# A planner's order for ScalarE and VectorE: from hand-set slacks to deadlines worked back from TensorE

## The chip, the core and the metric

One core of a Trainium2 chip runs the kernel. TensorE multiplies, VectorE and ScalarE do the arithmetic between its products, GpSimd helps in the first third, and SP issues nearly all DMAs. The metric is the device time of one execution in microseconds; lower is better.

## The reference, cut to what matters

A causal attention with a decay feeds two feed-forward layers; the change lies in the second half of the kernel, in the layers.

```python
x = attn_out.transpose(0, 2, 1, 3).reshape(2304, 512)   # after the attention
h = x @ w_in                     # 512 -> 2048
x = (h - np.tanh(h)) @ w_out     # layer 0, 2048 -> 512
h = x @ w_in2
return (h * (1 / (1 + np.exp(-h)))) @ w_out2            # layer 1
```

The weights arrive as float64, and the kernel turns them into float32 on the chip.

## The kernel before

Each float32 operand is split into a high and a low part (`gr`, `xr`, `wh`/`wl`), and a product is three matmuls. Blocks of two by two are multiplied with seven products in place of eight (a Strassen-Winograd scheme), so sums of blocks are made on VectorE ahead of the products (the stages `f_a`, `f_b`, `f_12`, `f_21`, `f_22`) and of the weights (`ws`), and results are gathered in running sums in PSUM.

A *unit* is one of three blocks of 768 tokens with one of four sets of 512 hidden columns, in each of two layers: 24 units. The first three run in slots that are written out by hand; from 259 us on the function `joint` makes the rest. TensorE's order there is fixed: h step, a step, h step, a step. An h step (`h_step`, L656) multiplies an x block (`xr`) by the input weights into a PSUM bank `h`; an a step (`c_step`, L729, and `plain_c`, L769, for the three units of `PLAIN`) multiplies the bent hidden block (`gr`) by the output weights into a bank `a`. A unit has seven of each (eight a steps in a plain one), and its a steps run beside the next unit's h steps.

Between them stand, on ScalarE, the copies that seed one running sum with another (`h<-h` L937, `a<-a` L1016), the activations (L930, L933), the casts to the high parts (`gr` L980, `xr` L905, `wh` L247) and the scaling of raw weights (L203); on VectorE the low parts (`gr` L981, `xr` L902, `wl` L249), the sums of stages (L940), h - tanh(h) (L934), the decoding of weights (L207 to L230) and the results' sums (`x<-a,x` L1024). In the last set of layer 0 four more sums per unit (`mix`, L1047) read the bank `a` and mix quarters of x. `make` (L890 to L905) prepares the `xr` of layer 1 and spills them to DRAM.

`joint` only lists tasks: a due time in steps of TensorE, an engine (P TensorE, A ScalarE, V VectorE, S and D DMAs), a cost in steps, what is read and written, a flag `keen` and an addend `spare`. `planned` runs the list against a clock of its own: TensorE and the DMAs keep their order; VectorE and ScalarE take, whenever they come free, one of the tasks that are ready. The order in which tasks come out is the order in which instructions are issued, and each engine works through its own strictly. In the rule of before the task with the least `when + spare` is taken; a task that isn't keen gives way to a keen one that becomes ready while it would run:

```python
n = min(now, key=lambda n: tasks[n][7])
if not tasks[n][6] and tasks[n][7] > t - 2:
    soon = [r for r, k in known if tasks[k][6] and t < r < t + tasks[n][2] - 0.2]
```

SP issues the reloads of `xr` (L625), the spills (L638), the weights (L164) and `aside` (L673, L676), a block of sums parked in DRAM, in the order of the tasks that they stand behind.

Of the kernel before, what the change touches and what calls it, by code (L numbers as in the profile page):

```python
# [8 lines left out]
F32R = mybir.dt.float32r  # L9
# [5 lines left out]
P = 128  # L15
# [24 lines left out]
PLAIN = (12, 13, 14)  # L40
PLAINSETS = {u // NB for u in PLAIN if u >= NB * NSET}
EARLIER = 5
MIXED = {u // NB for u in PLAIN if u < NB * NSET}

# [4 lines left out]
def forgetting_attention_two_ffn(  # L49
# [106 lines left out]
    def wload(q, m, parts=(0, 1)):  # L156
# [20 lines left out]
    )  # L177
# [418 lines left out]
    def ftile(u, what):  # L596
        k = u % 2
        if what == "12":
            if "12" not in small_tiles:
                small_tiles["12"] = pools["xb"].tile([P, 2, 2, TH], F32, tag="xo7", name="f_12")  # L600
            return small_tiles["12"][:, k]
        if what == "21":
            return flat(f"21_{k}", "hp", f"h{k}")
        if what == "1":
            return flat("1", "tp", "t0")
        if what == "22":
            return flat("22", "tp", "t1")
        if what == "tmp":
            if what not in small_tiles:
                g = gfree.pop(0)  # L610
                small_tiles[what] = pools[f"gp{g // 2}"].tile([P, 2, TH], F32, tag=f"gh{g}", name="f_tmp")
                small_tiles["spare"] = g
            return small_tiles[what]
        return flat(what, "xt", {"a": "xt1", "b": "xt2"}[what])
# [49 lines left out]
    def aside_tile():  # L664

        if "tile" not in aside:
            g = small_tiles["spare"]
            aside["tile"] = pools[f"gp{g // 2}"].tile([P, 2, TH], F32, tag=f"gl{g}", name="aside")
        return aside["tile"]
# [40 lines left out]
    def c_step(u, k):  # L710
        l, i = units[u][0], csteps(u)[k]
        t = gtile(gop(u, k))
        if u in PLAIN:
            return plain_c(u, *i, t)
        acc, fresh = cbank(u, i)
        at = WAT[l][i]
        ws = [[w[:, 0] for w in place(2 * (u // NB) + j, at)] for j in range(2)]
        for d in range(3 if l else 2):
            ds = slice(d * P, d * P + P)
            for j, (wh, wl) in enumerate(ws):  # L720
                gh, gl = (t[:, e, j] for e in range(2))
                if l:
                    dst = acc[:, d // 2, 256 * (d % 2):256 * (d % 2) + 256]
                    terms = ((gh[:, ds], wh), (gh[:, ds], wl), (gl[:, ds], wh))
                else:
                    dst = acc[:, d, 0:TH]
                    terms = ((wh[:, ds], gh), (wh[:, ds], gl), (wl[:, ds], gh))
                for r, (w, m) in enumerate(terms):
                    nc.tensor.matmul(  # L729
                        dst, w, m, start=fresh and (l == 0 or d != 1) and j == r == 0,  # L730
                        stop=j == 1 and r == 2, skip_group_check=True,
                    )

    def place(q, at):

        if at >= 11:
            if q % NSLOT < 2:
                return [w[:, 7:8] for w in wtile(q, 0)]
            if "spare" not in wtiles:
                g = small_tiles["spare"]  # L740
                t = pools[f"gp{g // 2}"].tile([P, 2, 256], F32R, tag=f"gl{g}", name="wspare")
                wtiles["spare"] = [t[:, 0:1], t[:, 1:2]]
            return wtiles["spare"]
        return [w[:, at - 8:] for w in extra(q, 1)] if at >= 8 else [w[:, at:] for w in wtile(q, 1)]
# [5 lines left out]
    def plain_c(u, c, a, t):  # L750
# [4 lines left out]
        for d in range(2 - a if l else 2):  # L755
            for j in range(2):
                q = 2 * (u // NB) + j
                gh, gl = (t[:, e, j] for e in range(2))
                if l:
                    ds = slice((2 * a + d) * P, (2 * a + d) * P + P)  # L760
# [35 lines left out]
    def joint():  # L796
# [5 lines left out]

        def task(when, eng, cost, fn, reads=(), writes=(), keen=False, spare=0):

            tasks.append((when, eng, cost, fn, reads, writes, keen, when + spare))

# [16 lines left out]
        def decode(q, m):  # L823
# [17 lines left out]
            groups = [0, 1, 2] if m and q // 2 in MIXED else [0, 1]  # L841
            behind = m and q % 2 and 3 * (q // 2) - 1 in PLAIN
            for g in [1, 3, 4, 5] if behind else groups:
# [4 lines left out]
        def spread(t0, t1, jobs, since):  # L848
# [3 lines left out]
            for e, c, fn, r, w, tag in jobs:  # L852
                if e == "D":
                    task(t - 6, e, c, fn, r, w)
                    continue
                t = max(t, since.get((w[0][:3], tag), t))
                task(t, e, c, fn, r, w, False, 3)
                if e == "V":
                    t += (t1 - t0) * c / total
# [22 lines left out]
        def make(u):  # L882
# [6 lines left out]
            def total(when, to, p, r, op=MINUS):  # L889
                task(t0 + when, "V", W2, lambda: tt_(q[to](), q[p](), q[r](), op), (key[p], key[r]), (key[to],), False, 2)  # L890

# [4 lines left out]
            for k, i in enumerate(STEPS):  # L896
# [7 lines left out]

                task(when, "A", N2, lambda n=n, f=f: copy(ring_tile(n)[:, 0], q[f]()), (key[f],), (kr,), False, 2)  # L905
                task(when + 0.1, "V", W2, low, (key[f], kr), (kr,), False, 2)


        for u in range(U0, len(units) + 1):
            t0 = base[u]  # L910
            if u < len(units):
# [27 lines left out]
                def two(when, to, p, r, op, kt, kp, kr, keen=True):  # L939
                    task(when, "V", W2, lambda: tt_(to, p, r, op), (kp, kr), (kt,), keen, 0 if keen else 2.5)  # L940

# [34 lines left out]
                for k, i in enumerate(order):  # L976
                    n = opno(u) + k
                    g, (frm, kf), kg = gtile(n), src[i], n % 3
                    w = t0 + when[k] + (more if k else 0)
                    task(w, "A", N2, lambda g=g, f=frm: copy(g[:, 0], f), (kf,), (("gh", kg),), False, 2)  # L980
                    task(w + 0.1, "V", W2, lambda g=g, f=frm: tt_(g[:, 1], f, rd(g[:, 0]), MINUS),  # L981
                         (kf, ("gh", kg)), (("gl", kg),), False, 2)
            v = u - 1
# [19 lines left out]
            for k, i in enumerate(csteps(v)):  # L1003
                if plain_:
                    n, kd = gop(v, k), (ky, kz)[i[1]]
                    r = [kd, ("gh", n % 3), ("gl", n % 3)] + [w for j in range(2) for g in (range(1) if l else range(3)) for w in wkeys(q + j, 1, g)]
                    task(t0 + min(2 * k + 1, 14), "P", 1, lambda v=v, k=k: c_step(v, k), r, (kd,))
                    continue
# [3 lines left out]
                when = t0 + k if last else t0 + 2 * k + 1  # L1012
                task(when, "P", 1, lambda v=v, k=k: c_step(v, k), r, (kd,))

# [15 lines left out]
            if l == 0:  # L1030
# [14 lines left out]
                else:  # L1045
                    def mix(when, spare, to, frm, r, op, keys, kt):
                        task(when, "V", W2, lambda: tt_(to() if callable(to) else to, frm, r, op), keys, (kt,), False, spare)  # L1047

                    mix(t0 + 11.5, 4, aside_tile, xs[22], xs[21], MINUS, (kx[22], kx[21]), "aside")
                    mix(t0 + 12.5, 3, xs[22], xs[22], xs[12], PLUS, (kx[22], kx[12]), kx[22])  # L1050
                    mix(t0 + 14.05, 1.2, xs[12], xs[12], ys, MINUS, (kx[12], ky), kx[12])
                    mix(t0 + 14.06, 1.2, xs[21], xs[21], ys, PLUS, (kx[21], ky), kx[21])
                task(t0 + (14.5 if s < NSET - 1 else 13), "S", 0, lambda b=b: aside_store(b), ("aside",), (("t1", b),))
# [62 lines left out]
    def planned(tasks):  # L1116
# [12 lines left out]
        writer, readers, deps = {}, {}, []  # L1129
        for n, (when, eng, cost, fn, reads, writes, keen, due) in enumerate(tasks):  # L1130
            d = {writer[k] for k in reads if k in writer}
# [11 lines left out]
        queue = {e: [n for n, t in enumerate(tasks) if t[1] == e] for e in free}  # L1143

        def ready(n):
            if all(d in end for d in deps[n]):
                return max([end[d] + lag(n, d) for d in deps[n]] + [tasks[n][0] - EARLY])

        while any(queue.values()):
            best = None  # L1150
            for e, waiting in queue.items():
# [457 lines left out]
```

## Time and profile before

| | |
|---|---|
| median of 3 runs | 914.43 us (914.15 to 914.65) |
| the profiled execution, its span | 914.77 us, 913.0 us |
| TensorE busy | 897.7 us, 98% |
| VectorE busy | 771.3 us, 84% |
| ScalarE busy | 594.6 us, 65% |
| DMA, mean | 215 GB/s |
| TensorE's granted clock, mean | 0.996 |

Times in the rows are microseconds from the span's start. A clock of 1.00 is 2.4 GHz, 0.50 is 1.2 GHz. An instruction of VectorE lasts in its row longer than the distance to the next one's start, since neighbours overlap a little; sums over a queue go by the starts.

### The profile page before, as it was taken

Reading aid. Unit: us, or ns where it says so; the run is one execution under the profiler, and the core shown is the slowest. Engines: PE = TensorE matmul, PEld = TensorE weight load, DVE = VectorE, ACT = ScalarE, POOL = GpSimd, SP = SyncE. Lnnn points to the kernel's source line nnn. Section 1 sums busy time; section 2 is a strip of 40 time slices with the busy share of each in tenths; the row PEclk is TensorE's granted clock in tenths of the full one; section 3 lists DMA queues with packets and bytes.
Section 4 is the critical chain, followed back from the end, with each engine's and each line's share of the span. In section 5 each row is a group of like instructions: output and inputs, shape, how many; then the busy total and the mean of one; then the engine's idle time right before and its main releaser. Section 6 shows DMA issues by size and latency. Waiting matters only on the chain.

```text
span 913.0 us, 15853 instructions
## 1 busy us (share of the span) xinstructions
PE 897.7 (98%) x5898; PEld 842.2 (92%) x5898; DVE 771.3 (84%) x1297; ACT 594.6 (65%) x992; POOL 161.3 (18%) x242
## 2 busy tenths in 40 slices
PE   9999999999999999999999989999999999999997
PEld 6777777799999999999999979898899999999997
DVE  7799999789888999998999989875598889876647
ACT  5888888766565767666776767665565566555443
POOL 8999999400000000000000000000000000000000
PEclk9999999999999999999999989999999999999999
DMA  5424533567457777787768656676567666555753
GB/s 164 154 98 155 167 121 103 193 245 314 196 217 265 237 252 259 236 302 280 251 241 287 220 207 252 238 267 235 190 230 282 205 225 225 180 201 176 233 167 117
DMA packets 51101, 196.01 MB, mean 215 GB/s; under 512 B 9744, under 2 KB 15120, under 8 KB 50992
## 3 DMA queue, kind: packets, MB, share of 16 engines
q1 hardware_dynamic: 50744, 194.72, 60.2%
q8 instruction: 46, 0.75, 0.3%
q10 hardware_dynamic: 280, 0.28, 0.1%
q14 instruction: 31, 0.25, 0.1%
HBM read 151.98 MB, written 41.88 MB: 212 GB/s over the span
## 4 chain that ended last, share of the span: by engine, by line
PE 93%; DVE 4%; ACT 2%; issue 1%; POOL 0%; DVEq 0%; ACTq 0%; POOLq 0%
PE h L656 32%; PE a L729 28%; PE a L769 5%; PE s L1294 5%; PE t L1341 5%; PE a L431 5%; PE out_t L1397 5%; PE h L475 3%; PE s L1286 2%; PE h L461 1%; PE out_t L1425 1%; DVE x L1047 1%; DVE gr L981 0%; DVE x L1024 0%; PE out L1397 0%
## 5 line engine op out<-in xcount | busy, mean ns | idle before, releaser
L656 PE MATMUL h<-xr,wh 128*128 128x384 f32 x1176 | 299.8, 335 | 1.0 <-ACT h L937 0.9
L656 PEld LDWEIGHTS h<-xr,wh 128*128 128x128 f32 x1176 | 210.6, 189 | 3.4 <-ACT h L937 1.6
L656 PE MATMUL h<-xr,wl 128*128 128x384 f32 x588 | 197.0, 335 | 0.0
L656 PEld LDWEIGHTS h<-xr,wl 128*128 128x128 f32 x588 | 110.6, 188 | 0.0
L981 DVE TENSOR_TENSOR gr<-f,gr 128x768 fp32r<-128x768 f32 x102 | 97.0, 953 | 14.5 <-ACT gr L980 14.5
L980 ACT CAST gr<-f 128x768 fp32r<-128x768 f32 x102 | 85.5, 838 | 33.3 <-PE a L729 29.5
L1024 DVE TENSOR_TENSOR x<-a,x 128x768 f32<-128x768 f32 (+1 forms) x64 | 59.4, 930 | 28.2 <-PE a L729 27.7
L1315 ACT ACTIVATE p<-p,mn 128x128 f32<-128x128 f32 (+3 forms) x128 | 71.2, 558 | 17.1 <-DVE mn L1307 14.4
L729 PE MATMUL a<-wh,gr 128*128 128x256 f32 x420 | 80.8, 282 | 0.0
L729 PE MATMUL a<-gr,wh 128*128 128x384 f32 x288 | 75.2, 341 | 4.7 <-ACT a L1016 4.1
L1329 POOL TENSOR_SCALAR p<-p,sm 128x128 f32<-128x128 f32 (+3 forms) x128 | 72.7, 584 | 7.7 <-DVE sm L1326 7.2
L1307 DVE CUSTOM_DVE_ANT_0 p<-s,mask 128x128 f32<-128x128 f32 (+3 forms) x128 | 59.6, 479 | 14.3 <-PE s L1294 14.2
L729 PEld LDWEIGHTS a<-wh,gr 128*128 128x128 f32 x420 | 67.5, 190 | 0.0
L1016 ACT COPY a<-a 128x768 f32<-128x768 f32 x43 | 33.7, 784 | 41.8 <-PE a L729 38.5
L729 PE MATMUL a<-weh,gr 128*128 128x256 f32 x312 | 60.2, 282 | 0.3 <-DVE x L1024 0.3
L729 PE MATMUL a<-wl,gr 128*128 128x256 f32 x210 | 59.4, 283 | 0.6 <-DVE wl L249 0.6
L937 ACT COPY h<-h 128x768 f32<-128x768 f32 x42 | 32.9, 784 | 39.6 <-PE h L656 39.2
L729 PEld LDWEIGHTS a<-gr,wh 128*128 128x128 f32 x288 | 53.0, 191 | 5.9 <-ACT a L1016 4.8
L729 PE MATMUL a<-gr,weh 128*128 128x384 f32 x216 | 54.8, 334 | 0.0
L1236 POOL TENSOR_TENSOR kqs<-kqraw,kqs 128x288 fp32r<-128x288 f32 (+1 forms) x62 | 53.8, 889 | 1.3
L937 ACT COPY f<-h 128x768 f32<-128x768 f32 x42 | 33.7, 802 | 30.4 <-PE h L656 22.7
L729 PEld LDWEIGHTS a<-weh,gr 128*128 128x128 f32 x312 | 50.2, 190 | 0.6 <-issue 0.5
(167 smaller groups left out, 2106.3 us busy)
## 6 DMA issues: line engine op xcount, KB each, us to landing
xr<-xd SPq DMA_DIRECT2D x126, 768.0 KB
raw<-w_in SPq DMA_DIRECT2D x32, 512.0 KB
raw<-w_out SPq DMA_DIRECT2D x32, 512.0 KB
xd<-xo SPq DMA_DIRECT2D x21, 768.0 KB
xd<-xr SPq DMA_DIRECT2D x21, 768.0 KB
kqraw<-kq SPq DMA_DIRECT2D x16, 608.0 KB
aside<-aside SPq DMA_DIRECT2D x15, 384.0 KB
vraw<-v SPq DMA_DIRECT2D x16, 320.0 KB
```

The costliest lines, as they stand in the source:

```text
L431: nc.tensor.matmul(dst, w, m, start=first and r == 0, stop=last and r == 2)
L656: nc.tensor.matmul(dst[:, j, 0:TH], w[:, ds], m[:, d], start=i in (1, 5) and d == r == 0, stop=d == 1 and r == 2, skip_group_check=True,)
L729: nc.tensor.matmul(dst, w, m, start=fresh and (l == 0 or d != 1) and j == r == 0, stop=j == 1 and r == 2, skip_group_check=True,)
L769: nc.tensor.matmul(dst, w, m, start=fresh and j == r == 0, stop=last and j == 1 and r == 2, skip_group_check=True)
L937: task(when, "A", N2, lambda: copy(to, frm), (kf,), (kt,), True)
L980: task(w, "A", N2, lambda g=g, f=frm: copy(g[:, 0], f), (kf,), (("gh", kg),), False, 2)
L981: task(w + 0.1, "V", W2, lambda g=g, f=frm: tt_(g[:, 1], f, rd(g[:, 0]), MINUS), (kf, ("gh", kg)), (("gl", kg),), False, 2)
L1024: task(when, "V", n, lambda: tt_(to, *((frm, to) if op == PLUS else (to, frm)), op), (kf, kx[c]), (kx[c],), True)
L1236: eng.tensor_tensor(lo[:, c0:c1], raw[p][:, c0:c1], rd(hi[:, c0:c1]), ALU.subtract)
L1307: nc.vector.tensor_tensor_reduce(out=pt.rearrange("p (g c) -> p g c", g=2) if i == 4 else pt, in0=src, in1=m, op0=ALU.add, op1=ALU.min, sc ...
L1315: nc.scalar.activation(pt, pt, AF.Exp, bias=mn, scale=-1.0, accum_out=sums[:, n // 3 % 5, n % 3, 0:1],)
L1329: nc.gpsimd.tensor_scalar(pt, pt, sm[:, j:j + 1], 1.0, ALU.mult, ALU.mult)
```

## The change

Every task loses `spare`. `planned` works a latest start back from TensorE's tasks through all that depend on each other, takes the ready task with the least latest start, and lets an engine idle for a more urgent task that is about to be ready, if the chosen one could wait for it. `behind` is how late TensorE's last planned step is against its due time. `keen` stays only in the planned lag of a dependence. The other edits concern sets of units that are plain in part (`MIXED`), the place of their weights, and a name (`spare` becomes `aside`).

```diff
-PLAINSETS = {u // NB for u in PLAIN if u >= NB * NSET}
+PLAINSETS = {s for s in range(NSET, 2 * NSET) if all(NB * s + b in PLAIN for b in range(NB))}
-MIXED = {u // NB for u in PLAIN if u < NB * NSET}
+MIXED = {u // NB for u in PLAIN} - PLAINSETS
...
-        def task(when, eng, cost, fn, reads=(), writes=(), keen=False, spare=0):
+        def task(when, eng, cost, fn, reads=(), writes=(), keen=False):
 
-            tasks.append((when, eng, cost, fn, reads, writes, keen, when + spare))
+            tasks.append((when, eng, cost, fn, reads, writes, keen))
...
-                task(t, e, c, fn, r, w, False, 3)
+                task(t, e, c, fn, r, w)
...
-                    mix(t0 + 14.05, 1.2, xs[12], xs[12], ys, MINUS, (kx[12], ky), kx[12])
-                    mix(t0 + 14.06, 1.2, xs[21], xs[21], ys, PLUS, (kx[21], ky), kx[21])
+                    mix(t0 + 14.05, xs[12], xs[12], ys, MINUS, (kx[12], ky), kx[12])
+                    mix(t0 + 14.06, xs[21], xs[21], ys, PLUS, (kx[21], ky), kx[21])
...
+        latest = [t[0] if t[1] == "P" else 1e9 for t in tasks]
+        for n in reversed(range(len(tasks))):
+            for d in deps[n]:
+                if tasks[d][1] != "P":
+                    latest[d] = min(latest[d], latest[n] - lag(n, d) - tasks[d][2])
...
+        behind = 0
...
-                n = min(now, key=lambda n: tasks[n][7])
-                if not tasks[n][6] and tasks[n][7] > t - 2:
-                    soon = [r for r, k in known if tasks[k][6] and t < r < t + tasks[n][2] - 0.2]
-                    if soon:
-                        t = min(soon)
-                        n = min((k for r, k in known if r <= t and tasks[k][6]), key=lambda n: tasks[n][7])
+                n = min(now, key=lambda n: latest[n])
+
+                soon = [(r, k) for r, k in known if t < r < t + tasks[n][2] - 0.1 and latest[k] + behind < t + tasks[n][2]
+                        and latest[n] + behind > r + tasks[k][2]]
+                if soon:
+                    t, n = min(soon)
...
+            if e == "P":
+                behind = t - tasks[n][0]
```

In the orders below L numbers are those of each kernel's own file, and names carry their buffer and tile numbers. The first place is the turn from layer 0 to layer 1, 523 to 531 us. `x_69<-x_69,a0` are the two `mix` sums that read the bank, `gr0` is the low part that an a step waits for, `xr64` to `xr66` are blocks of layer 1. VectorE before:

```order
L934 TENSOR_TENSOR f_21_1_3814<-h1_3809,f_21_1_3814 128x768
L902 TENSOR_TENSOR xr64_6064<-x_69,xr64_6064 128x768
L890 TENSOR_TENSOR f_tmp_4038<-x_69 128x768
L940 TENSOR_TENSOR f_a_3815<-f_12_3812,f_1_3811 128x768
L1047 TENSOR_TENSOR aside_4345<-x_69 128x768
L940 TENSOR_TENSOR f_12_3812<-f_22_3813,f_12_3812 128x768
L1047 TENSOR_TENSOR x_69<-x_69,a0_3795 128x2x384
L1047 TENSOR_TENSOR x_69<-x_69 128x2x384
L902 TENSOR_TENSOR xr65_6134<-f_tmp_4038,xr65_6134 128x768
L1047 TENSOR_TENSOR x_69<-x_69,a0_3795 128x2x384
```

VectorE now:

```order
L912 TENSOR_TENSOR xr64_6065<-x_69,xr64_6065 128x768
L1058 TENSOR_TENSOR x_69<-x_69 128x2x384
L944 TENSOR_TENSOR f_21_1_3814<-h1_3809,f_21_1_3814 128x768
L944 TENSOR_TENSOR f_12_3812<-f_12_3812,f_tmp_4039 128x768
L1058 TENSOR_TENSOR x_69<-x_69,a0_3795 128x2x384 x2
L900 TENSOR_TENSOR f_tmp_4039<-x_69 128x768
L991 TENSOR_TENSOR gr0_3817<-f_21_1_3814,gr0_3817 128x768
L950 TENSOR_TENSOR f_a_3815<-f_12_3812,f_1_3811 128x768
L950 TENSOR_TENSOR f_b_3816<-f_22_3813,f_a_3815 128x768
L912 TENSOR_TENSOR xr65_6156<-f_tmp_4039,xr65_6156 128x768
```

The two sums that read `a0` stand now next to each other, three rows behind `f_21_1`, where they stood six and nine rows behind it, and `f_a` stands behind them. ScalarE at the same place, before:

```order
L937 COPY h1_3809<-h0_3810 128x2x384
L905 CAST xr65_6134<-f_tmp_4038 128x768
L905 CAST xr66_6140<-x_69 128x768
L980 CAST gr2_3819<-f_a_3815 128x768
L930 ACT_TABLE_LOAD
L930 ACTIVATE f_1_3811<-h1_3809 128x768
L905 CAST xr67_6162<-x_69 128x768
L1016 COPY a0_3795<-a1_3802 128x2x384
L980 CAST gr1_3818<-f_b_3816 128x768
```

ScalarE now:

```order
L947 COPY h1_3809<-h0_3810 128x2x384
L915 CAST xr66_6139<-x_69 128x768
L1027 COPY a0_3795<-a1_3802 128x2x384
L915 CAST xr65_6156<-f_tmp_4039 128x768
L940 ACT_TABLE_LOAD
L940 ACTIVATE f_1_3811<-h1_3809 128x768
L990 CAST gr1_3818<-f_b_3816 128x768
L990 CAST gr2_3819<-f_a_3815 128x768
```

`a0<-a1` stood behind the table load and two more, and stands now ahead of the table load. The second place is the end of the plain units, 650 to 657 us, on ScalarE; `wh2_1` are weight blocks of the a steps to come, `x_69<-a0` and `x_69<-a1` are results of the last plain unit. Before:

```order
L930 ACTIVATE f_21_1_3814<-h1_3809 128x768
L980 CAST gr1_3818<-f_21_1_3814 128x768
L1065 COPY x_69<-a1_3802 128x2x256
L1065 COPY x_69<-a0_3795 128x2x512
L980 CAST gr2_3819<-f_b_3816 128x768
L247 CAST wh2_1_3854<-ws11_1_6862 128x256
L937 COPY h1_3809<-h0_3810 128x2x384
L247 CAST wh2_1_3854<-ws11_1_6862 128x512
L247 CAST wh2_1_3854<-ws11_1_6862 128x256
```

Now:

```order
L940 ACTIVATE f_21_1_3814<-h1_3809 128x768
L990 CAST gr1_3818<-f_21_1_3814 128x768
L1076 COPY x_69<-a1_3802 128x2x256
L247 CAST wh2_1_3854<-ws11_1_6863 128x256
L1076 COPY x_69<-a0_3795 128x2x512
L247 CAST wh2_1_3854<-ws11_1_6863 128x512
L947 COPY h1_3809<-h0_3810 128x2x384
L990 CAST gr2_3819<-f_b_3816 128x768
L247 CAST wh2_1_3854<-ws11_1_6863 128x256
```

The first cast of `wh2_1` moved ahead of the result `x_69<-a0`, and `gr2` behind it and two others; the scaling of raw weights went further back. The third place is VectorE at a turn within layer 0, 377 to 384 us; `gr1<-f_21_0` is the first `gr` of the new unit, `wb6_1`, `wel2` and `wl2_1` belong to the decoding of weights. Before:

```order
L230 TENSOR_TENSOR ws5_1_4766<-ws5_1_4766 128x256
L249 TENSOR_TENSOR wl2_1_3855<-ws5_1_4766,wh2_1_3854 128x1024
L940 TENSOR_TENSOR f_a_3815<-f_12_3812,f_1_3811 128x768
L211 TENSOR_SCALAR wb6_1_4875<-wa6_1_4834 128x1024
L940 TENSOR_TENSOR f_12_3812<-f_22_3813,f_12_3812 128x768
L940 TENSOR_TENSOR f_b_3816<-f_22_3813,f_a_3815 128x768
L981 TENSOR_TENSOR gr1_3818<-f_21_0_3820,gr1_3818 128x768
L249 TENSOR_TENSOR wel2_3872<-ws5_1_4766,weh2_3871 128x512
```

Now:

```order
L944 TENSOR_TENSOR f_22_3813<-f_22_3813,f_tmp_4039 128x768
L944 TENSOR_TENSOR f_21_0_3820<-h0_3810,f_21_0_3820 128x768
L214 SCALAR_TENSOR_TENSOR wb6_1_4837<-raw6_1_4729,wb6_1_4837 128x1024
L944 TENSOR_TENSOR f_12_3812<-f_12_3812,f_tmp_4039 128x768
L249 TENSOR_TENSOR wel2_3872<-ws5_1_4767,weh2_3871 128x512
L249 TENSOR_TENSOR wel2_3872<-ws5_1_4767,weh2_3871 128x256
L950 TENSOR_TENSOR f_a_3815<-f_12_3812,f_1_3811 128x768
L991 TENSOR_TENSOR gr1_3818<-f_21_0_3820,gr1_3818 128x768
```

A row of decoding and both `wel` stand now ahead of `gr1`, and `f_12` and `f_b` behind it; `wl2_1` went further ahead.

## Rows read from the trace of the kernel before

**Rows 1.** The page, part 1: busy time, share of the span, instructions of each engine.
```profile
PE 897.7 (98%) x5898; PEld 842.2 (92%) x5898; DVE 771.3 (84%) x1297; ACT 594.6 (65%) x992; POOL 161.3 (18%) x242
```

**Rows 2.** TensorE's waits, 283 to 913 us: total, times, longest us.
```profile
PE a L729 <- ACT a L1016: 4.1, 2, 3.7
PE a L729 <- DVE wl L249: 0.6, 1, 0.6
PE a L729 <- DVE gr L981: 0.6, 1, 0.6
PE h L729 <- DVE gr L981: 0.4, 1, 0.4
```

**Rows 3.** The chain that ended last: start us, duration us, what, instructions.
```profile
383.48 2.26 PE a L729 x12
...
489.74 2.10 PE h L656 x12
...
500.61 2.35 PE a L729 x12
...
517.52 2.08 PE a L729 x12
...
519.60 2.09 PE h L656 x12
...
538.81 2.90 PE h L656 x12
...
650.03 4.14 PE a L769 x18
...
659.26 2.08 PE h L656 x12
...
889.98 2.16 PE a L729 x18
...
897.10 4.33 PE a L729 x36
```

**Rows 4.** Windows, 535 to 540 us: PE, PEld, DVE, ACT, POOL busy; PEclk; DMA; GB/s.
```profile
535.00:540.00 5.00, 5.00 (x16) 5.00 (x17) 3.63 (x5) 1.25 (x2) 0.00 (x0) 0.50 0.39 157
```

**Rows 5.** Timeline of ScalarE, 525 to 534 us: start, duration, line, what [idle before].
```profile
525.87 0.78 ACT L937 COPY h<-h 128x768 f32<-128x768 f32 x1 [1.49 <-PE h L656]
...
530.08 1.28 ACT L930 ACT_TABLE_LOAD   x1 [1.20 <-PE h L656]
531.38 0.81 ACT L930 ACTIVATE f<-h 128x768 f32<-128x768 f32 x1
...
532.80 0.80 ACT L1016 COPY a<-a 128x768 f32<-128x768 f32 x1
533.53 0.83 ACT L980 CAST gr<-f_b 128x768 fp32r<-128x768 f32 x1
```

**Rows 6.** Timeline of VectorE, 516 to 535 us.
```profile
516.35 0.95 DVE L902 TENSOR_TENSOR xr<-x,xr 128x768 fp32r<-128x768 f32 x1
...
522.56 0.96 DVE L934 TENSOR_TENSOR f<-h,f 128x768 f32<-128x768 f32 x1 [0.30 <-ACT f L933]
...
530.38 0.95 DVE L1047 TENSOR_TENSOR x<-x,a 128x768 f32<-128x768 f32 x1
531.24 0.95 DVE L940 TENSOR_TENSOR f_b<-f,f_a 128x768 f32<-128x768 f32 x1
...
533.91 0.95 DVE L981 TENSOR_TENSOR gr<-f,gr 128x768 fp32r<-128x768 f32 x1
```

**Rows 7.** Groups of VectorE by form: count, busy us, mean ns, idle before.
```profile
L214 DVE SCALAR_TENSOR_TENSOR wb<-raw,wb 128x1024 f32<-128x1024 uint32 x29 | 35.5, 1223 | 0.6
```

**Rows 8.** Timeline of ScalarE near 656 us.
```profile
655.83 0.41 ACT L247 CAST wh<-ws 128x256 fp32r<-128x256 f32 x1
```

**Rows 9.** Timeline of VectorE near 383 us.
```profile
383.40 1.03 DVE L249 TENSOR_TENSOR wel<-ws,weh 128x512 fp32r<-128x512 f32 x2
```

**Rows 10.** SP's queue, waits, 283 to 913 us.
```profile
SPq L676 <- DMA aside<-aside: 28.3, 6, 5.8
```

More of the change, by code (lines that the diff above doesn't have):

```diff
@@ L611, in ftile @@
                 small_tiles[what] = pools[f"gp{g // 2}"].tile([P, 2, TH], F32, tag=f"gh{g}", name="f_tmp")
-                small_tiles["spare"] = g
+                small_tiles["aside"] = g
             return small_tiles[what]
@@ L666, in aside_tile @@
         if "tile" not in aside:
-            g = small_tiles["spare"]
+            g = small_tiles["aside"]
             aside["tile"] = pools[f"gp{g // 2}"].tile([P, 2, TH], F32, tag=f"gl{g}", name="aside")
@@ L715, in c_step @@
         acc, fresh = cbank(u, i)
+        if k == 0 and l and units[u - 1][0] == 0:
+            w = place(2 * (u // NB), WAT[l][i])[0][:, 0]
+            for c in range(2):
+                nc.tensor.matmul(csums(u)[1][:, 0, 256 * c:256 * c + 256], t[:, 0, 0, 0:P], w, start=c == 0, stop=True,
+                                 skip_group_check=True)
         at = WAT[l][i]
@@ L736, in place @@
         if at >= 11:
[L737 to L743, printed above, removed]
+            return [w[:, 7:8] for w in wtile(min(q % NSLOT, 1), 0)]
         return [w[:, at - 8:] for w in extra(q, 1)] if at >= 8 else [w[:, at:] for w in wtile(q, 1)]
@@ L758, in plain_c @@
                 gh, gl = (t[:, e, j] for e in range(2))
+                if l and u // NB in MIXED:
+                    ds = slice((2 * a + d) * P, (2 * a + d) * P + P)
+                    for k, at in enumerate(((11, 1), (0, 2))[i]):
+                        wh, wl = (w[:, 0] for w in place(q, at))
+                        for r, (w, m) in enumerate(((gh[:, ds], wh), (gh[:, ds], wl), (gl[:, ds], wh))):
+                            nc.tensor.matmul(
+                                acc[:, d, 256 * k:256 * k + 256], w, m, start=fresh and j == k == r == 0,
+                                stop=last and j == 1 and r == 2, skip_group_check=True,
+                            )
+                    continue
                 if l:
@@ L841, in decode @@
             groups = [0, 1, 2] if m and q // 2 in MIXED else [0, 1]
-            behind = m and q % 2 and 3 * (q // 2) - 1 in PLAIN
+            behind = m and l and q % 2 and 3 * (q // 2) - 1 in PLAIN and q // 2 not in MIXED
             for g in [1, 3, 4, 5] if behind else groups:
@@ L889, in total @@
             def total(when, to, p, r, op=MINUS):
-                task(t0 + when, "V", W2, lambda: tt_(q[to](), q[p](), q[r](), op), (key[p], key[r]), (key[to],), False, 2)
+                task(t0 + when, "V", W2, lambda: tt_(q[to](), q[p](), q[r](), op), (key[p], key[r]), (key[to],))
             task(t0 - 4, "D", 3, lambda: aside_load(b, q["11"]()), (("t1", b),), (key["11"],))
@@ L903, in low @@
                     spill(n)
-                task(when, "A", N2, lambda n=n, f=f: copy(ring_tile(n)[:, 0], q[f]()), (key[f],), (kr,), False, 2)
-                task(when + 0.1, "V", W2, low, (key[f], kr), (kr,), False, 2)
+                task(when, "A", N2, lambda n=n, f=f: copy(ring_tile(n)[:, 0], q[f]()), (key[f],), (kr,))
+                task(when + 0.1, "V", W2, low, (key[f], kr), (kr,))
         for u in range(U0, len(units) + 1):
@@ L939, in two @@
                 def two(when, to, p, r, op, kt, kp, kr, keen=True):
-                    task(when, "V", W2, lambda: tt_(to, p, r, op), (kp, kr), (kt,), keen, 0 if keen else 2.5)
+                    task(when, "V", W2, lambda: tt_(to, p, r, op), (kp, kr), (kt,), keen)
                 cp(t0 + 1.05, zs, ys, kz, ky)
@@ L979, in joint @@
                     w = t0 + when[k] + (more if k else 0)
-                    task(w, "A", N2, lambda g=g, f=frm: copy(g[:, 0], f), (kf,), (("gh", kg),), False, 2)
+                    task(w, "A", N2, lambda g=g, f=frm: copy(g[:, 0], f), (kf,), (("gh", kg),))
                     task(w + 0.1, "V", W2, lambda g=g, f=frm: tt_(g[:, 1], f, rd(g[:, 0]), MINUS),
-                         (kf, ("gh", kg)), (("gl", kg),), False, 2)
+                         (kf, ("gh", kg)), (("gl", kg),))
             v = u - 1
@@ L1005, in joint @@
                     n, kd = gop(v, k), (ky, kz)[i[1]]
-                    r = [kd, ("gh", n % 3), ("gl", n % 3)] + [w for j in range(2) for g in (range(1) if l else range(3)) for w in wkeys(q + j, 1, g)]
+                    r = [kd, ("gh", n % 3), ("gl", n % 3)] + [w for j in range(2) for g in (range(1) if q // 2 in PLAINSETS else range(3)) for w in wkeys(q + j, 1, g)]
                     task(t0 + min(2 * k + 1, 14), "P", 1, lambda v=v, k=k: c_step(v, k), r, (kd,))
@@ L1012, in joint @@
                 when = t0 + k if last else t0 + 2 * k + 1
-                task(when, "P", 1, lambda v=v, k=k: c_step(v, k), r, (kd,))
+                kd = (kd, kz) if k == 0 and v == NB * NSET and v - 1 not in PLAIN else (kd,)
+                task(when, "P", 1, lambda v=v, k=k: c_step(v, k), r, kd)
             def seed(when):
@@ L1045, in joint, with mix @@
                 else:
[L1046 to L1050, printed above, removed]
-                    mix(t0 + 14.05, 1.2, xs[12], xs[12], ys, MINUS, (kx[12], ky), kx[12])
-                    mix(t0 + 14.06, 1.2, xs[21], xs[21], ys, PLUS, (kx[21], ky), kx[21])
+                    def mix(when, to, frm, r, op, keys, kt):
+                        task(when, "V", W2, lambda: tt_(to() if callable(to) else to, frm, r, op), keys, (kt,))
+                    mix(t0 + 11.5, aside_tile, xs[22], xs[21], MINUS, (kx[22], kx[21]), "aside")
+                    mix(t0 + 12.5, xs[22], xs[22], xs[12], PLUS, (kx[22], kx[12]), kx[22])
+                    mix(t0 + 14.05, xs[12], xs[12], ys, MINUS, (kx[12], ky), kx[12])
+                    mix(t0 + 14.06, xs[21], xs[21], ys, PLUS, (kx[21], ky), kx[21])
                 task(t0 + (14.5 if s < NSET - 1 else 13), "S", 0, lambda b=b: aside_store(b), ("aside",), (("t1", b),))
@@ L1129, in planned @@
         writer, readers, deps = {}, {}, []
-        for n, (when, eng, cost, fn, reads, writes, keen, due) in enumerate(tasks):
+        for n, (when, eng, cost, fn, reads, writes, keen) in enumerate(tasks):
             d = {writer[k] for k in reads if k in writer}
```

2 rows, old and new, of the table GROUPS are left out of this document.

## The prediction

> **What bounds the kernel now.** I read the page's busy times first: TensorE is busy for 897.7 of 913.0 us, VectorE 84% and ScalarE 65% [rows 1]. So only time in which TensorE waits, or runs slow, can be won, and the next view is its waits behind 283 us, where the two orders first part: 4.1 us for ScalarE's copy a<-a, and 0.6, 0.6 and 0.4 us for VectorE [rows 2]. Waits alone understate the loss, so the third view is the chain, in which TensorE's steps stand with their starts. A step of 12 matmuls takes 2.08 us, one of 18 in the second layer 2.16. Steps follow each other without a gap nearly everywhere; where they don't, count the steps between two rows and compare [rows 3]:
> - From 519.60 to the end of the step of 538.81 (541.71) stand 7 steps: 7 x 2.08 = 14.56, but 22.11 passed: 7.55 us lost.
> - From 489.74 to the end of the step of 500.61 (502.96) 6 steps: 12.48, but 13.22 passed: 0.74 lost.
> - The step of 650.03 ends at 654.17; 2.08 and 2.16 later is 658.41, and the next h step starts at 659.26: 0.85 lost.
> - From 889.98 three steps of 2.16 end at 896.46; the next starts at 897.10: 0.64 lost.
> - The step of 383.48 takes 2.26: 0.18 lost.
>
> The first is larger than its waits (3.7 us is the longest) because TensorE then runs at the lower level: from 535 to 540 us the granted clock is 0.50, which is 1.2 GHz [rows 4], after TensorE had waited 3.7 us. So about half of the 7.55 is the wait and half the slow steps behind it; who removes the wait gets both.
>
> **The change part by part.** The diff's other edits (the sets MIXED and PLAINSETS, the fixed sum for a set half plain, the place of a spare weight) do nothing for PLAIN = (12, 13, 14): that set is the whole set 4, so PLAINSETS and MIXED come out as before, and none of the new branches is reached. No instruction is added or removed; TensorE's order is unchanged. What is left is the order on VectorE and ScalarE, and the DMAs that stand behind their instructions.
>
> *The stall at 530.* TensorE waits for a<-a, which overwrites a bank that VectorE's two x<-x,a (L1047) must have read. Before, nine instructions stand on VectorE from f_21 (522.56) to the second x<-x,a (530.38), each 0.87 after the last; then a<-a is queued on ScalarE behind a table load, f<-h (to 532.19) and a cast, and starts at 532.80 [rows 5, 6]. Last comes gr0<-f_21, at 533.91. In the new order f_21 is the eighth row behind xr63 (516.35): if none waits, it starts at 516.35 + 8 x 0.87 = 523.31, 0.75 later than before, but the second x<-x,a starts 3 rows behind it, at 525.92, and ends at 526.87. On ScalarE a<-a now stands behind h<-h (525.87 to 526.65) and one cast of 0.83, so it runs from about 527.5 to 528.3. gr0 is the fifth row behind f_21: 527.66 to 528.6. The step is due at 519.60 + 5 x 2.08 = 530.00: 1.4 us to spare. The wait goes, and no slow clock follows it.
>
> What is late next? The h step due at 532.08 needs xr65, the eighth row behind f_21: 530.27 to 531.22, 0.9 to spare. The step due at 534.16 needs gr1<-f_b: its cast stands on ScalarE behind the table load (530.08, 1.28) and f<-h, which ends at 532.19 as before, since both wait for the same TensorE step; cast to 533.02, then VectorE 533.05 to 534.00. That is 0.16 to spare, the narrowest place. I count the whole 7.55, and keep 1 us of lateness here as an upper end of its cost.
>
> The table load is the one place where a rule speaks against this. The row has 1.28 us, and f<-h starts 0.02 behind its end [rows 5]. The Trainium skill (ScalarE: Activation LUTs, What ACT_TABLE_LOAD costs) gives 1283 ns for the load and about 1380 ns of drain, 2.66 us for a switch. The trace agrees with the load and shows no drain between it and the next instruction. By the page's whole figure gr1 would come 1.2 us behind its step and the sum would be 1.2 smaller.
>
> *The stall at 500* is the same turn one unit earlier: four reads and mixes of x, and a<-a behind them. In the new order both x<-x,a stand ahead of f_a, f_12 and f_b, three instructions of 0.87, so a<-a is free to start when its TensorE step ends, and the 0.74 goes. Below: nothing gained, if the decode rows now pulled ahead of them (1.22 us each) [rows 7] eat it up.
>
> *The wait at 656* is for a weight block, wl<-ws,wh, whose cast (0.41 us, 655.83) stands behind x<-a and gr [rows 8]. It now stands first behind the step that frees its buffer (654.17), and ends by 654.6, ahead of the whole step that reads it, which begins at 656.25. The 0.85 goes. Queued behind the cast's new wait are x<-a and the rest; each is 0.4 later, and the step behind needs h<-h only at 658.41.
>
> *The end.* gr<-f_a stands behind an x<-a,x that waits for TensorE; now it stands ahead of it. The 0.64 goes; the chain of stores behind the last step stays.
>
> *A turn that gets worse, 383.* Ahead of gr1<-f_21 there now stand a decode step wb<-raw,wb (1.22) and both wel (1.03), and f_b and f_12 are behind it. With 0.08 of overlap each: 1.14 + 0.95 - 2 x 0.87 = 0.35 later [rows 6, 7, 9]. gr1 ended the wait there already, so the step loses 0.35 more. VectorE's other turns in the first layer also come closer to their limits; in each I set the growth of the work ahead of a TensorE input against its lead over its step, and found nothing else over by more than 0.1.
>
> *The queues.* Spills and weight loads move by one to four rows on SP. One could matter: the spill of xr64 stands now behind the store and load of aside; such a load has waited 5.8 us at the longest [rows 10]. By the count above xr64 ends at 522.52, and the buffer that its spill frees is needed again only by xr67, for the step due at 540.40. Some 10 us cover it, so I cost it at nothing; without that cover it would cost its whole wait.
>
> **The sum.** 7.55 + 0.74 + 0.85 + 0.64 - 0.35 = 9.43 us. The profiled execution took 914.77 (span 913.0 and 1.8 around it), 0.34 over the median of 914.43; so 905.3 in its terms, and 905.0 beside the median. All that I listed, with the 0.18 at 383 won and not 0.35 lost, would be 9.96: 904.5.
>
> **The rivals.**
> - *The next input is late.* xr65 or gr1<-f_b misses its step at 532 to 534 by 1 us, perhaps both do, and the clock falls for a few steps; a table switch longer than its row is one way to it. For: 0.16 to spare. Against: a 128x768 instruction of VectorE takes 0.95 or 0.96 us in each of its rows [rows 6]. Price 1.5 to 4 (two waits of 1 us, and as much again at half the clock): 906.5 to 909.
> - *VectorE is the bound of the first layer.* Its turns from unit to unit are packed; nine of them, 29.1 us (14 steps of 2.08) apart, stand behind 283 us, two of which are the stalls above. If each of the other seven lost 0.35, as worked out for 383, it is 2.5 at most: 907.5; with 0.8 each 5.6: 910.6. For: VectorE is 84% busy over the span, and only in these turns does TensorE wait for it. Against: 383 is the only one that the count finds late.
> - *The same, past break-even: slower.* With 1.3 us lost at each of the nine turns, 11.7 in all, the gain of 9.43 is used up and the kernel takes 916.7. It decides from the point where a turn has more than 1.05 us of VectorE work added ahead of its gr, about one decode row of 1.14, beyond its lead. For: at 383 one did. Against: there two rows of 0.87 moved behind, and elsewhere growth stays under the lead.
> - *The change doesn't do what it says.* The plan's steps are all of one length, and it plans waits by fixed lags; where the chip differs, the stall only moves, with its slow clock: 911 to 915. Against: the count above uses the chip's own times, and leaves 1.4 us.
>
> **How the numbers follow.** Forecast, 904.3 to 907: 0.72. Next input late: 0.10. Crowded turns: 0.11. Stall moved: 0.05. Slower: 0.02. A measurement of this kernel can tell about 0.2%, 1.8 us, from no change, so faster means under 912.6 and slower over 916.3. Faster takes the first three and a little of the fourth, 0.94; same most of the fourth, 0.04; slower 0.02. The range goes from 903.8 (all of it won, and 0.7 of gaps too short for the list) to 909.2, which takes in the first rival and most of the second.
>
> **What would show it.** Right: no clock of 0.50 in any stretch behind 283 us; a<-a near 528 and TensorE's step at 530.00 by the old times; waits for a<-a under 0.5 us in total; the chain with TensorE alone from 490 to 560; a step near 383 of 2.6 us. Wrong: a new wait over 0.5 us for gr, xr or f of VectorE at a turn, a second stretch at 1.2 GHz, or an xr load from DRAM that lands behind its step.

## The result and the profile after

The changed kernel takes 905.39 us (median, 904.8 to 906.37), the kernel before 914.36 on the same chip: a ratio of 0.9903, with a 95% interval of 0.9886 to 0.992. In a second comparison (run `again` below) it took 904.63, ratio 0.9896 (0.9878 to 0.9914). The forecast was 905.0. Two executions lie far outside all others and are left out of every median and ratio here: one of `t530b` with 3119.26 us, whose steps of TensorE took 7.4 us each at a granted clock of 1.00 in the record, and one of the kernel before beside `again` with 2273.16; no run shows what they are.

The page of after, part 1, which answers to [rows 1]:

```profile
PE 892.5 (99%) x5898; PEld 839.0 (93%) x5898; DVE 768.7 (85%) x1297; ACT 591.7 (66%) x992; POOL 161.5 (18%) x242
```

TensorE has 5.2 us less of busy time with the same 5898 matmuls, and no stretch at half the clock any more. VectorE and ScalarE are busy for 2.6 and 2.9 us less. The span is 902.7 us, 10.3 less than in the profile of before. That profile is one of the longer executions of before: beside the later runs its executions have spans of 911.3 to 913.8 us, 912.1 in the middle, while those of the changed kernel have 902.7 to 903.4. So 9.3 us of span is the usual gain.

TensorE's waits in after, 283 to 913 us, against [rows 2] (line 735 was 729, 1035 was 1024):

```profile
PE a L735 <- DVE x L1035: 0.3, 1, 0.3
```

All four lines of [rows 2] are gone; this one, at the kernel's end, is in before too (there `PE a L729 <- DVE x L1024: 0.3, 1, 0.3`). The chain of after, at the places of [rows 3]:

```profile
383.15 2.08 PE a L735 x12
...
499.63 2.08 PE a L735 x12
...
526.67 2.08 PE h L656 x12
528.75 2.08 PE a L735 x12
530.83 2.08 PE h L656 x12
...
645.35 2.10 PE h L656 x12
647.45 2.15 PE a L735 x18
649.60 2.08 PE h L656 x12
...
886.80 4.33 PE a L735 x36
```

Each of these steps starts where the one ahead of it ends: there is no gap at the places that were 383, 500, 530 and 656 before (the last now stands at 647.45, and the h step of 659.26 at 649.60), and at the end the step of 886.80 takes its 4.33 with nothing lost ahead of it. I took the length of each of TensorE's steps from 259 us on, less the usual length of its kind, and added these up: 11.42 us of loss before, 1.45 after. So 9.97 of the 10.3 us were won at the five places on the list. The remaining 0.33 is no gain of the change: TensorE's steps stand 0.33 us earlier from the first 20 us on (the step of 383.48 starts at 383.15), as they do in b383, which is built on the kernel before, and behind the last step 4.58 us pass in both.

The window of [rows 4] in after, same columns:

```profile
535.00:540.00 5.00, 5.00 (x30) 5.00 (x30) 5.00 (x8) 4.34 (x6) 0.00 (x0) 1.00 0.44 177
```

The clock stays at 1.00, its level of 2.4 GHz. The timelines of ScalarE and VectorE in after, against [rows 5, 6]:

```profile
524.63 0.78 ACT L947 COPY h<-h 128x768 f32<-128x768 f32 x1 [0.76 <-PE h L656]
...
526.71 0.78 ACT L1027 COPY a<-a 128x768 f32<-128x768 f32 x1 [0.55 <-PE a L735]
...
528.82 1.28 ACT L940 ACT_TABLE_LOAD   x1 [0.58 <-PE h L656]
530.12 0.81 ACT L940 ACTIVATE f<-h 128x768 f32<-128x768 f32 x1
530.83 0.82 ACT L990 CAST gr<-f_b 128x768 fp32r<-128x768 f32 x1
```
```profile
523.78 1.81 DVE L1058 TENSOR_TENSOR x<-x,a 128x768 f32<-128x768 f32 x2
...
526.38 0.95 DVE L991 TENSOR_TENSOR gr<-f,gr 128x768 fp32r<-128x768 f32 x1
...
529.10 0.95 DVE L912 TENSOR_TENSOR xr<-f_tmp,xr 128x768 fp32r<-128x768 f32 x1
...
531.68 0.96 DVE L991 TENSOR_TENSOR gr<-f_b,gr 128x768 fp32r<-128x768 f32 x1 [0.76 <-ACT gr L990]
```

Both x<-x,a end at 525.59, and a<-a runs at 526.71, behind h<-h and one cast instead of behind the table load. By the old times of the step it waits for (1.25 us earlier here: 0.92 from the places won before it, and the 0.33 of the start) that is 528.0: the prediction had "near 528".

### The profile page after: what moved, and what is told of

Its sections match the earlier page's. It is cut to its first block, busy times and chain, and to the rows that moved or that the text cites. A ratio compares the mean times of both kernels' runs of the same rounds, so it can differ in the third digit from the quotient of the medians.

```text
span 902.7 us, 15866 instructions
## 1 busy us (share of the span) xinstructions
PE 892.5 (99%) x5898; PEld 839.0 (93%) x5898; DVE 768.7 (85%) x1297; ACT 591.7 (66%) x992; POOL 161.5 (18%) x242
## 4 chain that ended last, share of the span: by engine, by line
PE 95%; DVE 3%; ACT 1%; POOL 0%; issue 0%; DMA 0%; DVEq 0%; POOLq 0%; ACTq 0%
PE h L656 33%; PE a L735 29%; PE a L779 6%; PE t L1362 5%; PE s L1315 5%; PE a L431 5%; PE out_t L1418 5%; PE h L475 3%; PE s L1307 2%; PE h L461 1%; PE out L1418 0%; PE out_t L1446 0%; DVE x L1035 0%; ACT raw L203 0%; PE h L735 0%
## 5 line engine op out<-in xcount | busy, mean ns | idle before, releaser
L735 PE MATMUL a<-gr,wh 128*128 128x384 f32 x288 | 73.0, 334 | 0.0
```

Of the source, the lines that this page charges most:

```text
L735: nc.tensor.matmul(dst, w, m, start=fresh and (l == 0 or d != 1) and j == r == 0, stop=j == 1 and r == 2, skip_group_check=True,)
```

## The experiments

Most of them cut a stretch out of one plan and put it into the other. For this `planned` works out both, as one list of rows for each engine, `due` by the old rule and `late` by the new one; where both lists hold the same set of rows up to a place, they can be cut there. All rows of all engines are then issued in the order of the spliced lists. All runs but `again` are built on the kernel before, without the diff's other edits.

### The turn at 530 alone (t530), and with what stands behind it (t530b, t530c)

```diff
+rows = due
+rows["V"][293:324], rows["A"][213:225] = late["V"][293:324], late["A"][213:225]   # t530
+rows["V"][293:354], rows["A"][213:247] = late["V"][293:354], late["A"][213:247]   # t530b, t530c
```

> The old plan, with the new plan's order in the turn at 530 us alone: 31 rows of VectorE and 12 of ScalarE. My theory (the gain is that of single turns, and this one holds 7.55 us, wait and slow clock together): 914.4 - 7.55 = 906.8 us, 906.4 to 907.8, no stretch at a clock of 0.50 behind 283 us, and the small losses of 0.74, 0.85, 0.64 and 0.18 still there. Rival A (the gain is spread over the many small moves of the joint stage): 911 to 914. Rival B (the stall moves to the next input): 908 to 912.

Measured: 909.96 us, ratio 0.9954 (0.9939 to 0.9969). Only 4.0 us were won, not 7.55; the time lies in the range of rival B. The timeline of ScalarE in t530 behind the turn, and the next step of the chain:

```profile
533.92 1.15 ACT L203 ACTIVATE raw<-raw 128x1024 f32<-128x1024 f32 x1
536.24 0.83 ACT L980 CAST gr<-f 128x768 fp32r<-128x768 f32 x1 [1.17 <-DVE f L940]
536.97 0.79 ACT L937 COPY h<-h 128x768 f32<-128x768 f32 x1
```
```profile
537.82 3.69 PE h L656 x12
```

The stall at 530 is gone, but h<-h, for the step due at 536, stands behind a scaling of raw weights and a cast that waits for VectorE's f (1.17 us idle). In the new plan both stand behind it. So the piece was extended.

> The old plan with a longer piece of the new one: the turn at 530 us and what stands behind it up to 562 us, 59 rows of VectorE and 28 of ScalarE. In the shorter piece, of 909.96 us, 3.7 us of the loss came back at 536: ScalarE's copy h<-h stood there behind old rows, the scaling of raw weights (1.15 us) and a cast gr<-f that waits for VectorE. My theory (the turn reaches to those rows, and the stall is whole gone when they follow too): 914.0 - 7.55 = 906.4 us, 905.9 to 907.4, no clock of 0.50 to 0.85 behind 283 us. Rival (what is left in the shorter piece depends on the turns ahead of it, which are 1 us earlier in the new plan): 908.5 to 910.5.

Measured: 907.65 us as the median of three executions (906.98, 907.65, 908.72), ratio 0.993 (0.9913 to 0.9947), 0.25 above the expected range. The profiled execution is the one that is left out, so it ran once more.

> The old plan with the new order in the turn at 530 us and behind it to 562 us, once more, for its trace: in the first profile of it each of TensorE's steps took 7.25 us. Theory: 906.4 to 907.7 us, the steps from 526 to 562 us at 2.08, and the losses of 0.74, 0.85, 0.64 and 0.18 still there. Rival (some of the 7.55 comes back behind 562): a new wait of 0.5 to 1.2 us near 562.

Measured: 907.03 us, ratio 0.9924 (0.9908 to 0.9939). In its trace each step from 525 to 554 us takes 2.08, the clock is 1.00, and 3.80 us of loss are left of 11.42: 7.6 gone, nothing new behind 562, the other places as before. The term of 7.55 stands for the profiled execution of before; by the medians the piece wins 6.4 and 7.1 us. It belongs to the whole piece, which by the slices in the edit has 61 places of VectorE's list and 34 of ScalarE's, not to the few rows that my count named.

### The new plan with the old turn (x530)

```diff
+rows = late
+rows["V"][293:324], rows["A"][213:225] = due["V"][293:324], due["A"][213:225]
```

> The new plan, with the old plan's order in the turn at 530 us alone, the mirror of the run before. My theory: the stall and its slow clock come back whole, 905.4 + 7.55 = 912.9 us, 912.0 to 913.4, with a wait for a<-a of 3 to 3.7 us and a clock near 0.50 behind it. Rival A (spread): 905.4 to 908.

Measured: 912.29 us, ratio to before 0.9979 (0.9969 to 0.9988), 6.9 over the 905.39 of the changed kernel. TensorE's waits in x530:

```profile
PE a L729 <- ACT a L1016: 3.7, 1, 3.7
PE a L729 <- DVE gr L981: 0.6, 1, 0.6
PE h L656 <- DMA xr<-xd: 0.6, 1, 0.6
```

The stall is back as in [rows 2], with 7.2 us of loss from 527 to 541 us. It is less than 7.55 because the clock was low for a shorter time: the h step behind the stall takes 2.55 us here, 2.90 in before. The third wait is new, and the section on why the prediction was right takes it up with SP's queue.

### One half of the turn: VectorE's order (v530), the copy a<-a alone (a530)

```diff
+rows = due
+rows["V"][293:324] = late["V"][293:324]                       # v530
+rows["A"][213:225] = late["A"][213:225]                       # a530
+x = [653, 680, 661, 679]                                     # a530: aside<-x, x<-x,a, x<-x, x<-x,a
+rows["V"] = [n for n in rows["V"] if n not in x]              # a530
+at = rows["V"].index(662)                                     # a530: f_tmp<-x
+rows["V"][at:at] = x                                          # a530
```

> The old plan, with VectorE's 31 rows of the turn at 530 us in the new order and ScalarE's as before. My theory (the copy a<-a then still stands on ScalarE behind the table load, f<-h and a cast, and ends near 533.6 us): the wait of 3.7 us and the slow clock stay, only the 0.6 us for gr goes: 913.8 us, 913.0 to 914.5. Rival (VectorE's x<-x,a was the cause, and the rest follows it): 906.8 to 908.

Measured: 913.83 us, ratio 0.9999 (0.9989 to 1.0008). As expected: the wait for a<-a is 4.0 us, and a<-a ran at 532.85, behind table load, f<-h and a cast, as in [rows 5].

> The old plan, with only the copy a<-a freed: ScalarE's 12 rows in the new order, and on VectorE the two x<-x,a with the two rows that they need moved ahead of f_tmp<-x; gr<-f_21 stays where it was, 13 rows behind f_21, and ends near 534.9 us. My theory (two inputs of the step at 530.00 were late, a<-a at 533.6 and gr at 534.9): the step starts at 530 and waits some 4.2 us for gr after its first matmuls; nothing is won: 914.2 us, 913.4 to 914.8, and the clock falls to 0.50 as before. Rival (a<-a is the stall, as its 3.7 us in the list of waits reads): 914.4 less 5 to 7, 907.5 to 909.5.

Measured: 916.73 us, ratio 1.0027 (1.0018 to 1.0037). The rival is out; my own figure of 914.2 missed by 2.5. TensorE's wait and VectorE's rows in a530:

```profile
PE a L729 <- DVE gr L981: 5.8, 1, 5.8
```
```profile
522.96 0.96 DVE L934 TENSOR_TENSOR f<-f,f_tmp 128x768 f32<-128x768 f32 x1 [2.04 <-ACT f_tmp L933]
...
525.57 0.95 DVE L1047 TENSOR_TENSOR aside<-x 128x768 f32<-128x768 f32 x1
...
535.62 0.95 DVE L981 TENSOR_TENSOR gr<-f,gr 128x768 fp32r<-128x768 f32 x1
```

gr ends at 536.57, not near 534.9, since the row f<-f,f_tmp waited 2.04 us for an f_tmp that the new order has later on ScalarE. So some 1.7 us of this result come from the edit itself, and show that the two engines' lists go together; without them, by the same sum, the time would have been 915.0, no gain either. In the list of waits of [rows 2] a<-a has 3.7 us and gr 0.6; here a<-a is only 0.7 us late (it ended at 530.30), and the wait for gr is 5.8. Two inputs were late, by 3.7 and 4.9 us, and the list puts down to gr only what was left when a<-a had come.

### The clock's share of the stall (cover, cover33)

```diff
+        if (u, k) == (11, 1):
+            w = wtile(8, 0)[0][:, 0, 0:P]
+            for _ in range(54):                                # cover33: 33
+                nc.tensor.matmul(chain(12)[0][:, 0, TH:512], w, w, start=False, stop=True, skip_group_check=True)
```

> The kernel before, with 54 matmuls of 128 x 128 on TensorE in the stall at 530 us, between the step that ends at 530.00 and the one that waits for a<-a; they write columns of a bank that nothing reads, so nothing else changes. My theory (the clock fell because TensorE stood still): the two waits of 3.7 and 0.6 us stay, the clock stays at 1.00, and the slow steps' 3.3 us go: 913.9 - 3.3 = 910.6 us, 909.9 to 911.6. Rival (the clock falls for another reason, or the steps are slow for their inputs): 913.4 to 914.5; if the matmuls run past the wait they add up to 1 us.

Measured: 913.03 us, ratio 0.9988 (0.9978 to 0.9997). Only 1.0 us was won, not 3.3: the 54 matmuls took 5.98 us, longer than the stall. But in its trace the granted clock never fell behind 260 us, and the steps behind them took 2.15 and 2.08 us.

> The 54 matmuls in the stall took 111 ns each, 5.98 us, where the stall's two waits are 4.24: the steps behind them ran at a clock of 1.00 and took 2.08 each, but 1.8 us were added. Here 33 of them, 3.7 us. Theory (as before): the waits stay, the clock stays at 1.00, 914.0 - 3.3 = 910.7 us, 910.0 to 911.6. Rival (the slow steps have another cause): 913 to 914.5.

Measured: 912.51 us, ratio 0.9986 (0.9976 to 0.9995): 1.6 us won, half of what I expected (2.4 in the span of the profiled execution). The chain and a window of cover33 (PEclk is the third column from the end):

```profile
535.09 2.18 PE a L733 x11
537.27 2.08 PE h L656 x12
```
```profile
535.00:540.00 5.00, 4.91 (x28) 4.91 (x29) 5.00 (x7) 1.98 (x3) 0.00 (x0) 1.00 0.39 157
```

With TensorE kept busy the clock stays at 1.00 and the steps behind the stall take 2.08, against 0.50 in [rows 4]. So the fall came from the standstill, and the mechanism holds. In four of the ten executions it held only in part or not at all: six have a mean granted clock of 0.999 and 911.9 to 912.6 us, four have 0.997, as before, and 913.5 to 914.9. The size was off too: the step was due at 530.16 in this run and ends at 537.27, 7.11 later, which is 5.03 of loss. The wait is that for gr, to 535.05, and the 0.69 us in which TensorE ran one matmul between the two waits belongs to it. Of the 7.55 some 5.0 are the wait and 2.5 the clock.

### The key without the look ahead (key)

```diff
-                soon = [(r, k) for r, k in known if ...]
-                if soon:
-                    t, n = min(soon)
```

> The new plan's key (the latest time by TensorE's steps) without its look ahead: an engine takes the most urgent of what is ready, and never holds a place for a more urgent one. My theory (the key makes the gain, since at the turn at 530 us its rows are the same but for gr0 two rows later and h<-h ahead of a cast): 905.4 to 907.0, 906.0 us. Rival (the look ahead is needed: a row of 0.87 to 1.22 us that starts just ahead of an urgent one costs TensorE a wait at many turns): 908 to 912.

The lines of the edit are set against the new rule. Measured: 906.34 us, ratio 0.9913 (0.9896 to 0.9929). TensorE's waits in key:

```profile
PE a L729 <- DVE gr L981: 0.7, 2, 0.3
PE h L729 <- DVE gr L981: 0.4, 1, 0.4
```

The key makes nearly all of the gain, and since this run and `start` (904.22 us) change only the order, the diff's other edits have no part in it that can be seen. Without the look ahead three steps, of 474, 533 and 885 us, lose 0.61, 0.61 and 0.65: gr comes late there. At 533 it is gr1<-f_b, whose cast ScalarE ran behind that of f_a, so that VectorE ended it at 533.88 against 532.64 in after (0.5 of the difference is the loss at 474). This is the place that the prediction called the narrowest; in after 0.27 us were to spare.

### The turn at 383 alone (b383)

```diff
+rows = due
+rows["V"][125:163], rows["A"][85:104] = late["V"][125:163], late["A"][85:104]
```

> The old plan, with the new order in the turn at 383 us alone (35 rows of VectorE and 11 of ScalarE, from 371 us on). The prediction had the step of 383.48 lose 0.35 more there, and the new kernel lost nothing. Theory (the three rows gr, ws, ws that the new order puts ahead of f<-h,f cost 1.55 us here, and were free in the new kernel only because VectorE came to them earlier): f<-h,f starts at 372.4, gr ends 10.3 + 0.9 us later, and the step takes 2.26 + 0.13 = 2.39 us. By the prediction's count 2.61. Rival (the row order in the turn alone is enough): 2.08 to 2.15.

Measured: 917.81 us in one execution, where before has 914.03 as its median on that chip; the span is 915.0 against 913.0. VectorE's rows in b383:

```profile
370.36 0.42 DVE L230 TENSOR_TENSOR ws<-ws 128x256 f32<-128x256 f32 x1
...
371.90 1.82 DVE L940 TENSOR_TENSOR f<-h,f 128x768 f32<-128x768 f32 x2
...
382.18 0.96 DVE L981 TENSOR_TENSOR gr<-f,gr 128x768 fp32r<-128x768 f32 x1
```

Two ws sums and a gr stand ahead of f<-h,f as said. In the timeline of before, f<-h,f started at 371.04 and gr at 382.53, in a run whose steps stand 0.3 later (383.48 against 383.19): so f<-h,f is 1.15 later and gr where it was, and the step takes 2.29. So the prediction's 2.61 is out, and the turn's own order neither costs nor gains at this step; the a step of 387 loses 0.15 more. At 412 us, in the next unit's turn, TensorE waits 1.3 us for gr, a loss of 2.06 with the step of 418. My reading, which no run tests: decode rows pulled ahead push others onto the next turn, if that keeps the old order.

### The start (again, start)

```diff
+rows = late
+a = rows["A"]
+a.remove(23)                                  # h<-h of 271.80 us
+a.insert(min(a.index(40), a.index(53)), 23)   # ahead of gr<-f and of raw<-raw
```

> The changed kernel once more, beside the next one on the same chip. Its span fell by 10.3 us in the profiles and its time by 9.0 in the comparison, so the time around the span grew by 1. Theory (that difference is the scatter of single executions): 914.0 x 0.990 = 904.9 us, 904.3 to 905.5. Rival (the new order costs 1 us outside the span): 905.4 to 906.

Measured: 904.63 us; the four executions have spans of 902.7 to 902.9 and 1.8 to 2.0 us around them. The rival is out: what lay around the span in the first comparison was scatter.

> The changed kernel with one row moved at the beginning: ScalarE's h<-h of 271.80 us stands ahead of the second scaling of raw weights and a cast gr<-f, both of which it waited for. Theory (TensorE's wait of 1.1 us at 271.5, the largest that is left, goes): 1.1 to 1.2 us less than the changed kernel, 903.8 us if that takes 904.9, and a span of 901.5. Rival (the scaling, 1.1 us later, delays VectorE's decode rows, and the wait comes back in the next step): no difference, 904.5 to 905.5.

Measured: 904.22 us, ratio to before 0.9894 (0.9878 to 0.991), not to be told from the changed kernel. ScalarE in start:

```profile
271.14 0.78 ACT L937 COPY h<-h 128x768 f32<-128x768 f32 x1 [0.56 <-PE a L431]
271.84 1.18 ACT L203 ACTIVATE raw<-raw 128x1024 f32<-128x1024 f32 x1
...
273.64 1.48 ACT L449 COPY x<-a 128x768 f32<-128x768 f32 x2
```

h<-h is early and its step starts in time, but now x<-a stands behind the scaling, and the step behind waits for it. Half of the loss, 0.66 of 1.4, was won in the trace. This is the fastest version, by less than can be measured.

## Why the prediction was right

- *The stall at 530* (7.55): right in place, and in size for the profiled execution (7.6 in t530c). The spare was 0.78 us for xr65 and 0.27 for gr1, where I had 0.9 and 0.16. Two things in its reasoning were wrong. "About half of the 7.55 is the wait and half the slow steps" is 5.0 to 2.5. And the rows behind the turn belong to it: with the turn alone 3.7 of it came back at 536, the fourth rival ("the stall only moves"), which the whole plan avoids.
- *The stalls at 500, 656 and the end* (0.74, 0.85, 0.64): all gone; the trace of after alone shows how, since no run takes them one by one. At 500 a<-a starts at 497.59 and waits for TensorE only, where in before it started at 499.77, behind VectorE's x<-x,a. At the end gr<-f_a (881.95) runs ahead of the x<-a,x (882.82) that it stood behind. At 656 the gain is right and the reading was not: the cast of 0.41 us was to wait for the step that frees its buffer (654.17 in before, 645.35 in after), but it ran 2 us ahead of that step's end:

```profile
643.33 0.41 ACT L247 CAST wh<-ws 128x256 fp32r<-128x256 f32 x1
```

- *The turn at 383* (-0.35): wrong. The step lost 0.18 before and loses nothing after. The failed step is the count of "work ahead of gr" from f<-h,f at 371.04 on, a row that waited for TensorE and so had idle time ahead of it. In after three rows that stood behind it run ahead of it:

```profile
369.84 0.95 DVE L991 TENSOR_TENSOR gr<-f,gr 128x768 fp32r<-128x768 f32 x1
...
371.04 1.81 DVE L950 TENSOR_TENSOR f<-h,f 128x768 f32<-128x768 f32 x2
...
381.33 0.95 DVE L991 TENSOR_TENSOR gr<-f,gr 128x768 fp32r<-128x768 f32 x1
```

A gr (369.84) and two ws sums, 1.54 us, moved ahead of 371.04, and my count had not taken them off: 0.35 - 1.54 = -1.2, and gr starts 1.2 us earlier, at 381.33. b383 shows that the three rows were free only because the stretch ahead of them had been pulled forward as well.
- *SP's queue*, costed at nothing: right in both profiles of the changed kernel. But the 10 us of cover were worked out for the spill of xr64, and at another place, which the prediction passed over, there is hardly any. Waits of SP's queue, 460 to 490 us, in after and in x530:

```profile
SPq L676 <- DMA aside<-aside: 6.6, 1, 6.6
...
SPq L625 <- DMA xr<-xd: 0.8, 1, 0.8
```
```profile
SPq L676 <- DMA aside<-aside: 6.5, 1, 6.5
SPq L625 <- DMA xr<-xd: 2.3, 1, 2.3
```

The load of aside, and the loads of xr behind it, waited 6.6 us for the store (5.4 before); two loads of raw weights now stand just ahead of that store, where they stood behind the load. So the next xr is issued at 475.42, 1.9 us later than before (473.50), and its step starts at 480.91. In x530, whose rows there are those of the new plan, it was issued at 475.22 and landed 0.6 us late, and 0.85 were lost:

```profile
475.22 6.20 DMA xr<-xd
481.43 0.04 issue
481.47 2.36 PE h L656 x12
```

With 6.20 us it would have come late in after too; there it took 5.5 at most. Whether the order of these loads alone does it was not tried.
- *The sum*: 9.43 by the list with 383 as a loss; in the profiles the places gave 9.97, the figure that the prediction had named for the case that 383 is won, and 904.5 with it. 904.63 and 905.39 stand on both sides of the forecast, and that they lie so close to 905.0 is in part luck. The term at 383 was 0.53 too low, and the stall, sized from a profile with a long span, is smaller in the usual execution (6.4 and 7.1 us by the medians of t530b and t530c); the two errors work against each other.
- *The table load*: it took 1.28 us again and f<-h started 0.02 behind it. No trace here shows the drain that the Trainium skill (ScalarE: Activation LUTs, What ACT_TABLE_LOAD costs) adds to it; in v530 the cast ahead of the load ends at 530.11 and the load starts at 530.13.

## What to carry to other kernels

Read a stall with its list of what is late, not by the one input that the trace names: here a<-a and gr were late by 3.7 and 4.9 us, and freeing either one alone (a530, v530) gave nothing. When a greedy plan sets the order on several engines, a piece of a better plan need not bring its share of the gain: cut too short, it met old rows behind it, and lost to them (t530, b383). To count whether an input comes too late, start at the last place where the engine is idle in both orders, not at a row that happened to wait.

## What was not expected of the hardware

- Matmuls of 128 x 128 behind one another took 111 ns each at a granted clock of 1.00 (5.98 us for 54, in `cover`), while those of 128 x 384 take 173 (2.08 for 12): a third of the columns costs two thirds of the time.
- How long the clock stays low behind one and the same stall differs between executions: the h step behind it took 2.90 us in before, 2.55 in x530 and 3.00 in b383, against 2.08 at full clock.
